# X in token order and block-diagonal C of a chunked scan put into one tile and one load, with another order of the first zero fills, constants and loads

## The chip, the cores and the metric

The kernel is written by hand in Bass/Tile for Trainium2 and runs on one core. A core has five engines that run side by side and tell each other by semaphores when data is ready: TensorE (PE) multiplies matrices and writes to PSUM, VectorE (DVE) and ScalarE (ACT) work on elements, GpSimd (POOL) does slower element work and gathers, SyncE (SP) issues DMAs. Each engine runs its own instructions strictly in order. The metric is device time in microseconds (us) of one execution, lower is better.

## What is computed

Three stages, each fed by the one before: a chunked linear-attention scan, a mixture of experts that sends each token to one of 8 experts, and a wide MLP. The change lies in the first stage alone:

```python
# x (4, 8, 768, 32), a (4, 8, 768), B and C (4, 8, 768, 16); chunk = 32
for c in range(nc):
    sl = slice(c * chunk, (c + 1) * chunk)
    xc, Bc, Cc = (x[:, :, sl], B[:, :, sl], C[:, :, sl])
    la = log_a[:, :, sl]
    cum = np.cumsum(la, axis=-1)
    L = np.exp(cum[:, :, :, None] - cum[:, :, None, :])
    L = L * causal
    CB = np.einsum('bhin,bhjn->bhij', Cc, Bc)
    M = CB * L
    y_intra = np.einsum('bhij,bhjd->bhid', M, xc)
    decay_to_i = np.exp(cum)
    y_inter = np.einsum('bhin,bhnd->bhid', Cc, state) * decay_to_i[:, :, :, None]
    y[:, :, sl] = y_intra + y_inter
    ...
    state = decay_full[:, :, None, None] * state + np.sum(Bx, axis=2)
```

Then `x = y` as 3072 rows of 256, `_moe_ref` (gate, one expert of 256 x 1024 x 256 with relu, gate weight), and `_moe2_ref` (256 x 2048 x 256 with squared relu).

## The kernel before

**Tiling.** The scan's tokens are cut into 24 tiles of 128 tokens, i = 0 to 23, in six phases of four tiles (`ph = i // 4`). Even and odd phases use buffers 0 and 1 of the large tiles. A step, called here by a letter and its tile, is: S(i), L416, the products of C and B for a pair, 16 matmuls into `sc`; M(i), L419, `sc` times the decays `Qm`, on DVE; D(i), L435, 32 matmuls that make the state's update `dS` of two tiles; R(i), L452, eight small recurrences on DVE that make the states `st`; Y(i), L464 (M times x) and L471 (C times state), 16 matmuls each; row(i), L476, on DVE, which scales y into a row tile; then transposes (L493), the gate's logits (L502) and the gate (L526 to L564). `order()`, `gateB`, `spotA` and the like prepare the sending of tokens to experts.

**Operands.** A small matmul contracts over 128 partitions, and four chunks share them, so the operands are block-diagonal: a tile is filled with zeros once, and each phase's load writes only the blocks (`at` in `load_x`, partitions c, c+4, ... in `load_c`). `X2_p` holds X twice, in chunk order ([:, 0], read by Y) and in token order ([:, 1], read by D). `Cb_p` is the block-diagonal C that S reads, `CT_p` (three buffers) the transposed C that Y reads, `BB_p` (three) is B, `Bt_p` the scaled B that D reads and POOL writes in `prep`. A phase is loaded by 15 DMAs on SP: `load_b` 1, `load_x(ph, 1)` 4, `load_c` 4, `load_x(ph, 0)` 4, `load_t` 2. Of these X and C parts have 128 KB each. A load into a buffer waits for the last reader two phases back (for CT and BB, three), and each issue waits for the DMA eight issues before it to land.

**Start.** `aa` (the gates a) is loaded, clamped on DVE (L315), its logarithm taken on ACT (L316). Six matmuls (L331 to L341) make cumulative sums, ACT takes four exponentials of them (Fd, Q, Gm, Pd, L347 to L350), POOL makes Bt (L392) and Qm (L400) from Fd and Q, and D(0) and S(0) can run. The zero fills of phase 0 stand around that on DVE and POOL, those of phase 1 behind it on DVE, ACT and POOL (L631 to L636, L645 to L647).

**Order.** The schedule is by hand (`tc.manual_schedule()`): the order of the code is the order on each engine. The loop over i at L643 works S and D two tiles ahead: PE's order around phase 1 is D(0), S(0), S(1), D(2), Y(0), Y(1), Y(2), S(4), D(4), S(5), Y(3), D(6), Y(4), Y(5), S(8). Nothing of the stages behind waits for a clock time: the experts' weights are staged in the place of `Cb_0` from i = 18 (`ring.stage`, `ring.load`), and after i = 23 PE runs on through the experts and the MLP.

Of the kernel before, what the change touches and what calls it, by code (L numbers as in the profile page):

```python
# [244 lines left out]
def attention(tc, k, ctx):  # L245
# [59 lines left out]
    def zcopy(f, p, b):
        f(Cb[p][:, 2 * b:2 * b + 2].rearrange("p c b e f -> p (c b) (e f)"), zb)

    def xcopy(f, p, l, h):
        f(X2[p][:, l, 2 * h:2 * h + 2].rearrange("p c b f -> p (c b) f"), zb)
# [7 lines left out]
    g.memset(Cb[0][:, 2:4], 0.0)  # L317
    g.memset(X2[0][:, 0, 2:4], 0.0)
    v.memset(Bt[0], 0.0)
    xcopy(v.tensor_copy, 0, 0, 0)  # L320
    v.memset(CT[0][0:64, 1], 0.0)
    v.memset(CT[0][64:128, 0], 0.0)
    load_b(0)
    load_x(0, 1)
    load_c(0)
    load_x(0, 0)
# [1033 lines left out]
```

## Time and profile before

| | us |
|---|---|
| three timed runs | 529.36, 531.80, 532.12 (median 531.80) |
| the profiled execution, its own time | 529.87 |
| its span in the trace | 528.2 |
| PE, DVE, ACT, POOL busy | 503.2, 374.4, 260.9, 107.3 |
| mean granted clock of PE | 0.994 of full |

The span is 1.67 us shorter than the execution's own time. PE is busy nearly throughout, but a busy PE in the scan's part (up to about us 90) often waits for small results of DVE, and the chain of waits, which goes back from the last instruction to what released it each time, tells there what counts. In timelines a line is: start, duration, engine, source line, operation, out<-in, shape, count, and in brackets the idle time before and what ended it. Equal neighbours are merged, so a duration with x2 or more is that of the whole row.

### The profile page before, as it was taken

Reading aid. Unit: us, or ns where it says so; the run is one execution under the profiler, and the core shown is the slowest. Engines: PE = TensorE matmul, PEld = TensorE weight load, DVE = VectorE, ACT = ScalarE, POOL = GpSimd, SP = SyncE. Lnnn points to the kernel's source line nnn. Section 1 sums busy time; section 2 is a strip of 40 time slices with the busy share of each in tenths; the row PEclk is TensorE's granted clock in tenths of the full one; section 3 lists DMA queues with packets and bytes.
Section 4 is the critical chain, followed back from the end, with each engine's and each line's share of the span. In section 5 each row is a group of like instructions: output and inputs, shape, how many; then the busy total and the mean of one; then the engine's idle time right before and its main releaser. Section 6 shows DMA issues by size and latency. Waiting matters only on the chain.

```text
span 528.2 us, 11379 instructions
## 1 busy us (share of the span) xinstructions
PE 503.2 (95%) x4341; PEld 457.5 (87%) x4341; DVE 374.4 (71%) x827; ACT 260.9 (49%) x500; POOL 107.3 (20%) x127
## 2 busy tenths in 40 slices
PE   5978898999999999999999999999999999999994
PEld 3657777989999999999899997999999999999994
DVE  8987988858999899995667777665564555445462
ACT  3612336357565566653554544545454554544552
POOL 6852201443330220000000002002420320201021
PEclk9998999999999999999999999999999999999998
DMA  6777766757878765621001100000100100000010
GB/s 214 222 239 237 231 187 209 232 115 180 215 210 202 194 203 147 213 68 20 1 0 42 41 1 1 1 20 22 61 1 1 41 0 1 31 10 2 1 42 24
DMA packets 35884, 51.22 MB, mean 97 GB/s; under 512 B 7377, under 2 KB 26962, under 8 KB 35826
## 3 DMA queue, kind: packets, MB, share of 16 engines
q1 hardware_dynamic: 32706, 42.88, 28.4%
q0 software_dynamic: 2832, 7.01, 4.5%
q8 instruction: 36, 0.59, 0.4%
q10 hardware_dynamic: 288, 0.55, 0.3%
q14 instruction: 22, 0.18, 0.1%
HBM read 44.06 MB, written 6.37 MB: 95 GB/s over the span
## 4 chain that ended last, share of the span: by engine, by line
PE 69%; DVE 17%; issue 5%; ACT 3%; DMA 2%; POOL 1%; SPq 1%; POOLq 0%; DVEq 0%; ACTq 0%
PE u L1057 23%; PE h L1035 22%; PE h L902 10%; PE o L918 9%; DVE wlo L176 2%; DVE hl L907 2%; DVE st L452 2%; PE tpm L883 1%; DMA wst<-in_w_dram 1%; DMA Cb<-in_cc_dram 1%; PE y L471 1%; PE y L464 1%; DMA CT<-in_ct_dram 1%; POOL out_dram L1070 1%; DVE w L239 1%
## 5 line engine op out<-in xcount | busy, mean ns | idle before, releaser
L1042 DVE TENSOR_TENSOR gb<-q,ga 128x512 fp32r<-128x512 f32 (+1 forms) x112 | 69.6, 622 | 71.4 <-ACT ga L1041 66.4
L1041 ACT ACTIVATE ga<-q 128x512 fp32r<-128x512 f32 (+1 forms) x112 | 63.9, 571 | 99.4 <-DVE q L1040 99.4
L1057 PE MATMUL u<-woh,ga 128*128 128x256 f32 x384 | 108.5, 283 | 1.2 <-ACT ob L1069 0.6
L1057 PE MATMUL u<-wol,ga 128*128 128x256 f32 x384 | 108.1, 281 | 0.0
L1057 PE MATMUL u<-woh,gb 128*128 128x256 f32 x384 | 107.7, 280 | 0.4 <-DVE gb L1042 0.4
L1040 DVE TENSOR_TENSOR q<-r 128x512 f32<-128x512 f32 (+1 forms) x112 | 69.2, 618 | 37.5 <-ACT r L1039 36.5
L1035 PE MATMUL h<-zh,wih 128*128 128x512 f32 (+1 forms) x224 | 81.1, 362 | 0.0
L1035 PE MATMUL h<-zh,wil 128*128 128x512 f32 (+1 forms) x224 | 80.8, 361 | 0.0
L1035 PE MATMUL h<-zl,wih 128*128 128x512 f32 (+1 forms) x224 | 80.7, 360 | 0.0
L1057 PEld LDWEIGHTS u<-woh,ga 128*128 128x128 f32 x384 | 72.1, 188 | 5.9 <-ACT ga L1041 1.7
L1039 ACT ACTIVATE r<-h 128x512 f32<-128x512 f32 (+1 forms) x112 | 59.3, 530 | 33.3 <-PE h L1035 32.5
L1057 PEld LDWEIGHTS u<-wol,ga 128*128 128x128 f32 x384 | 72.1, 188 | 3.1
L1057 PEld LDWEIGHTS u<-woh,gb 128*128 128x128 f32 x384 | 72.5, 189 | 1.3 <-DVE gb L1042 1.2
L905 ACT ACTIVATE hh<-h 128x256 fp32r<-128x256 f32 (+8 forms) x72 | 34.1, 473 | 57.9 <-PE h L902 55.3
L1070 POOL DMA_INDIRECT out_dram<-ob,idx x24 | 24.8, 1033 | 131.4 <-ACT ob L1069 125.6
L1035 PEld LDWEIGHTS h<-zl,wih 128*128 128x128 f32 x224 | 42.1, 188 | 7.3
L907 DVE SCALAR_TENSOR_TENSOR hl<-h,hh 128x256 fp32r<-128x256 f32 (+8 forms) x72 | 38.1, 529 | 14.1 <-ACT hh L905 13.8
L918 PE MATMUL o<-hh,whi 128*128 128x256 f32 (+8 forms) x144 | 47.7, 331 | 0.0
L918 PE MATMUL o<-hh,wlo 128*128 128x256 f32 (+8 forms) x144 | 47.5, 330 | 0.2 <-DVE wlo L176 0.2
L918 PE MATMUL o<-hl,whi 128*128 128x256 f32 (+8 forms) x144 | 47.5, 330 | 0.1
L902 PE MATMUL h<-xh,whi 128*128 128x208 f32 (+7 forms) x128 | 44.6, 348 | 0.8 <-DVE hl L907 0.7
L1035 PEld LDWEIGHTS h<-zh,wil 128*128 128x128 f32 x224 | 42.0, 188 | 3.8
(210 smaller groups left out, 907.7 us busy)
## 6 DMA issues: line engine op xcount, KB each, us to landing
wst<-in_w_dram SPq DMA_DIRECT2D x64, 256.0 KB, 4.8
X<-in_xx_dram SPq DMA_DIRECT2D x48, 128.0 KB, 3.6
w<-in_win_dram SPq DMA_DIRECT2D x8, 512.0 KB, 6.4
w<-in_wout_dram SPq DMA_DIRECT2D x8, 512.0 KB, 3.8
xs<-row SPq DMA_DIRECT2D x6, 516.0 KB, 5.4
BB<-in_bb_dram SPq DMA_DIRECT2D x6, 512.0 KB, 4.7
Cb<-in_cc_dram SPq DMA_DIRECT2D x24, 128.0 KB, 3.6
CT<-in_ct_dram SPq DMA_DIRECT2D x12, 128.0 KB, 3.0
```

Source lines behind the costliest of these rows:

```text
L176: eng.tensor_tensor(lo[:, w], st[:, w], hi[:, w].bitcast(F32), ALU.subtract)
L902: nc.tensor.matmul(ps, ring.up(wt, e, f, kd), xt[:, kd], start=(i == 0), stop=(i == 5))
L905: nc.scalar.activation(a, ps, ACTF.Relu)
L907: rest = lambda: nc.vector.scalar_tensor_tensor(b, ps, 0.0, a.bitcast(F32), ALU.max, ALU.subtract)
L918: nc.tensor.matmul(self.yps[e][d][:, c:c + n], ring.down(wt, e, f, d), ht, start=(f == 0 and i == 0), stop=(f == 7 and i == 2))
L1035: nc.tensor.matmul(ps, wt[:, kd, m * 128:m * 128 + 128], zt[t][:, kd], start=(i == 0), stop=(i == 5))
L1039: nc.scalar.activation(r, ps, ACTF.Relu)
L1040: nc.vector.tensor_tensor(q, r, r, ALU.mult)
L1041: nc.scalar.activation(a, q, ACTF.Copy)
L1042: nc.vector.tensor_tensor(b, q, a.bitcast(F32), ALU.subtract)
L1057: nc.tensor.matmul(o, gt[:, q * 128:q * 128 + 128], wt[:, m], start=(m == 0 and i == 0 and h == 0), stop=(m == 15 and i == 2), skip_group_ ...
L1070: ins = nc.gpsimd.indirect_dma_start(out=k.out, out_offset=bass.IndirectOffsetOnAxis(ap=self.idx[:, c:c + 1], axis=0), in_=ob, in_offset=N ...
```

## The change

X in token order and the block-diagonal C become one DRAM array `xc` and one tile `XC_p` of 128 x 4 x 2048; a part is loaded by one DMA of 256 KB, so a phase has 11 DMAs where it had 15, with the same bytes. X in chunk order has an array `xa` and a tile `XA_p` of its own, 128 x 4 x 1024. The weights' staging takes the place of `XA_0` where it took that of `Cb_0`, and its loads stand at i = 19 instead of 18. The zero fills are dealt out anew: for phase 0 two quarters of `XC_0` to DVE, two to ACT, `XA_0` to POOL and DVE, `Bt_0` to POOL; for phase 1 all four quarters of `XC_1` and the four halves of CT to ACT, `XA_1` and `Bt_1` to POOL. The constants are loaded up to C_ID first, and the rest from ACT's queue behind Pd. The matmul that feeds Pd and Pd itself are a function `decay()`, called behind D(0). All loads of phase 1 stand ahead of the loop; `load_c` of phase ph + 2 comes at i % 4 == 0, `load_b(2)` and `load_t(2)` earlier.

```diff
-    s.dma_start(out=cst[:, 0:C_LO], in_=k.consts[:, 0:C_LO])
-    s.dma_start(out=cst[:, C_LO:C_END], in_=k.consts[:, C_LO:C_END])
+    s.dma_start(out=cst[:, 0:C_ID], in_=k.consts[:, 0:C_ID])
...
+    XC = [bigs[p].tile([128, 4, 2048], F32, name=f"XC_{p}") for p in range(2)]
+    XA = [(big if p else stp).tile([128, 4, 1024], F32, tag=f"XA_{p}", name=f"XA_{p}") for p in range(2)]
+    Xt = [x[:, :, 0:1024].rearrange("p c (b f) -> p c b f", b=2) for x in XC]
+    Cb = [x[:, :, 1024:2048].rearrange("p c (b e f) -> p c b e f", b=2, e=2) for x in XC]
+    Xr = [x.rearrange("p c (b f) -> p c b f", b=2) for x in XA]
...
-            sp.dma_start(out=Cb[p][c:128:4, c], in_=k.cc[ph, c:128:4])
+            sp.dma_start(out=XC[ph % 2][c:128:4, c], in_=k.xc[ph, c:128:4])
...
-    g.memset(X2[0][:, 1, 0:2], 0.0)
-    xcopy(v.tensor_copy, 0, 1, 1)
-    zcopy(v.tensor_copy, 0, 0)
+    load_b(0)
+    blank_c(v.tensor_copy, 0, 0)
+    g.memset(Bt[0], 0.0)
+    blank_c(acopy, 0, 2)
+    g.memset(XA[0][:, 0:2], 0.0)
+    blank_c(v.tensor_copy, 0, 1)
+    blank_c(acopy, 0, 3)
+    load_c(0)
     v.tensor_scalar(aa, aa, 1e-6, 1.0, ALU.max, ALU.min)
     s.activation(la, aa, ACTF.Ln)
...
+    def decay():
+        pe.matmul(cum[:, 1, :192], cst[:, C_WQ:C_WQ + 128], la[:, 1], start=True, stop=True)
+        s.activation(Pd.rearrange("p b t h -> p (b t h)"), cum[:, 1, :192], ACTF.Exp, scale=-1.0)
...
+    prep(0, (0,))
+    st_D(0)
+    decay()
+    s.dma_start(out=cst[:, C_ID:C_END], in_=k.consts[:, C_ID:C_END])
+    load_b(1)
+    for c in range(4):
+        blank_c(acopy, 1, c)
+    load_c(1)
+    prep(0, (1, 2))
+    for h in range(2):
+        g.memset(XA[1][:, 2 * h:2 * h + 2], 0.0)
+    load_x(1)
...
-            load_x(i // 4 + 2, 1)
+            load_c(i // 4 + 2)
...
         if i == 18:
-            k.ring.stage(stp, "Cb_0")
             k.moe = Moe(k, tc, k.c2, m0)
             k.ring.aim(0)
-            k.ring.load(0)
             k.moe.load_rows((0, 0))
...
         if i == 19:
+            k.ring.stage(stp, "XA_0")
+            for n in range(4):
+                k.ring.load(n)
```

ACT's first instructions (zt is the zero tile, Fd, Q, Gm and Pd the four exponentials, in words above), before:

```order
L265 DMA cst<-in_consts_dram 128x899
L266 DMA cst<-in_consts_dram 128x184
L316 ACT_TABLE_LOAD
L316 ACTIVATE aa<-aa 128x576
L347 ACT_TABLE_LOAD
L347 ACTIVATE Fd<-cu_163 128x192
L348 ACTIVATE Q<-cum 128x192
L349 ACTIVATE Gm<-small 128x96
L350 ACTIVATE Pd<-cum 128x192
L311 ACTIVATE Cb_120<-zt 128x2048
L311 ACTIVATE X_1_118<-zt 128x2048 x2
L311 ACTIVATE X_1_118<-zt 128x1024
```

and after:

```order
L264 DMA cst<-in_consts_dram 128x544
L304 ACT_TABLE_LOAD
L304 ACTIVATE XC_116<-zt 128x2048 x2
L326 ACT_TABLE_LOAD
L326 ACTIVATE aa<-aa 128x576
L354 ACT_TABLE_LOAD
L354 ACTIVATE Fd<-cu_166 128x192
L355 ACTIVATE Q<-cum 128x192
L356 ACTIVATE Gm<-small 128x96
L360 ACTIVATE Pd<-cum 128x192
L641 DMA cst<-in_consts_dram 128x539
L304 ACTIVATE XC_117<-zt 128x2048 x4
```

Two zero copies and a third table load came ahead of the logarithm, and four copies for phase 1 (`XC_117` is buffer 1) with a DMA issue stand behind Pd.

SP's queue from the second phase's loads on (`_117`, `_119`, `_124` are buffer 1 after the change; `Cb_119` and `X_0_117` are buffer 0 before it), before:

```order
L281 DMA BB_122<-in_bb_dram 128x1024
L286 DMA Cb_120<-in_cc_dram 32x1024 x4
L292 DMA X_1_118<-in_xx_dram 32x1024 x4
L641 DMA wg<-in_wg_dram 128x64
L292 DMA X_0_117<-in_xx_dram 32x1024 x4
L292 DMA X_1_118<-in_xx_dram 32x1024 x4
L296 DMA CT_125<-in_ct_dram 64x512 x2
L281 DMA BB_123<-in_bb_dram 128x1024
L286 DMA Cb_119<-in_cc_dram 32x1024 x4
```

and after:

```order
L283 DMA BB_121<-in_bb_dram 128x1024
L287 DMA XC_117<-in_xc_dram 32x2048 x4
L292 DMA XA_119<-in_xa_dram 32x1024 x4
L296 DMA CT_124<-in_ct_dram 64x512 x2
L283 DMA BB_122<-in_bb_dram 128x1024
L656 DMA wg<-in_wg_dram 128x64
L296 DMA CT_125<-in_ct_dram 64x512 x2
L287 DMA XC_116<-in_xc_dram 32x2048 x4
```

The third phase's X no longer stands ahead of the second phase's, CT of phase 2 comes ahead of phase 2's C, and four issues fewer stand in the row.

PE's first instructions, before:

```order
L331 MATMUL cu_163<-aa,cst 128x192
L334 MATMUL cu_163<-aa,cst 128x4x40
L336 MATMUL cum<-aa,cst 128x192
L337 MATMUL cum<-aa,cst 128x192
L340 MATMUL small<-aa,cst 128x96
L341 MATMUL small<-aa,cst 128x4x23
L435 MATMUL dS_129<-X_0_117,Bt_127 32x4x32 x8
L435 MATMUL dS_130<-X_0_117,Bt_127 32x4x32 x8
L416 MATMUL sc<-Cb_119,BB_121 32x256 x16
```

and after:

```order
L339 MATMUL cu_166<-aa,cst 128x192
L342 MATMUL cu_166<-aa,cst 128x4x40
L344 MATMUL cum<-aa,cst 128x192
L347 MATMUL small<-aa,cst 128x96
L348 MATMUL small<-aa,cst 128x4x23
L442 MATMUL dS_128<-XC_116,Bt_126 32x4x32 x8
L442 MATMUL dS_129<-XC_116,Bt_126 32x4x32 x8
L359 MATMUL cum<-aa,cst 128x192
L423 MATMUL sc<-XC_116,BB_120 32x256 x16
```

The second matmul into `cum` (that of Pd) moved behind D(0).

## Rows read from the trace of the kernel before

**Rows 1.** The page: shares of the chain of waits by engine.

```profile
PE 69%; DVE 17%; issue 5%; ACT 3%; DMA 2%; POOL 1%; SPq 1%; POOLq 0%; DVEq 0%; ACTq 0%
```

**Rows 2.** Chain of waits, first 10 us: start, duration, what.

```profile
3.73 2.82 DVE Cb L306
6.56 2.07 DVE aa L315
8.64 0.69 ACT aa L316
9.38 1.01 PE cu L331 x2
```

**Rows 3.** Timeline of PE: start, duration, line, operation, count, idle time before.

```profile
11.36 0.85 PE L337 MATMUL cum<-aa,cst 128*128 128x192 f32 x2
12.93 1.20 PE L435 MATMUL dS<-X,Bt 128*32 128x128 f32 x32
...
21.35 1.05 PE L416 MATMUL sc<-Cb,BB 128*32 128x256 f32 x16
...
28.75 0.65 PE L464 MATMUL y<-X,M 128*32 128x128 f32 x16 [0.96 <-DMA X<-in_xx_dram]
...
33.44 1.07 PE L416 MATMUL sc<-Cb,BB 128*32 128x256 f32 x16 [1.78 <-DMA Cb<-in_cc_dram]
...
43.72 0.50 PE L471 MATMUL y<-st,CT 128*32 128x128 f32 x8 [0.92 <-DMA CT<-in_ct_dram]
```

**Rows 4.** Timeline of ACT and of its DMA queue, first 20 us.

```profile
1.27 0.45 ACTq L266 DMA_DIRECT2D cst<-in_consts_dram  x1
...
9.35 1.28 ACT L347 ACT_TABLE_LOAD   x1
...
13.18 0.33 ACT L350 ACTIVATE Pd<-cum 128x192 f32<-128x192 f32 x1
13.39 1.92 ACT L311 ACTIVATE Cb<-zt 128x2048 f32<-128x2048 f32 x1
15.19 4.66 ACT L311 ACTIVATE X<-zt 128x2048 f32<-128x2048 f32 x3
```

**Rows 5.** Timelines of DVE (first row) and POOL (the others), zero fills.

```profile
9.61 1.16 DVE L309 COPY X<-zt 128x2048 f32<-128x2048 f32 x1
2.59 2.88 POOL L317 MEMSET Cb<- 128x2048 f32 x1
...
16.55 1.81 POOL L636 MEMSET X<- 128x2048 f32 x1
```

**Rows 6.** DMA issues of us 6.5 to 13, then 77 to 84: count, KB each, median to landing.

```profile
Cb<-in_cc_dram SPq DMA_DIRECT2D x4, 128.0 KB, 2.5
...
wst<-in_w_dram SPq DMA_DIRECT2D x8, 256.0 KB, 5.8
```

**Rows 7.** Timeline of DVE: row(5), M(8), M(12), M(16).

```profile
31.47 0.43 DVE L476 TENSOR_TENSOR row<-y,Pd 128x256 f32<-128x256 f32 x1 [0.88 <-PE y L471]
...
34.64 0.69 DVE L419 TENSOR_TENSOR M<-sc,Qm 128x512 f32<-128x512 f32 x1 [0.39 <-POOL Qm L400]
...
48.53 0.68 DVE L419 TENSOR_TENSOR M<-sc,Qm 128x512 f32<-128x512 f32 x1
...
60.17 0.68 DVE L419 TENSOR_TENSOR M<-sc,Qm 128x512 f32<-128x512 f32 x1
```

**Rows 8.** Stretches: length, busy us of PE, PEld, DVE, ACT, POOL, granted clock, DMA share, GB/s.

```profile
30.00:34.00 4.00, 2.22 (x65) 1.74 (x61) 2.85 (x9) 0.61 (x3) 3.21 (x8) 1.00 0.88 265
40.00:44.00 4.00, 2.65 (x46) 2.10 (x50) 2.75 (x10) 1.44 (x3) 0.00 (x0) 0.99 0.52 155
44.00:47.00 3.00, 3.00 (x57) 2.50 (x45) 0.78 (x3) 0.28 (x1) 0.00 (x0) 0.50 0.90 266
```

**Rows 9.** Timelines of PE (Y(19)) and of SP's queue (first weight load).

```profile
77.02 0.62 PE L464 MATMUL y<-X,M 128*32 128x128 f32 x16
...
77.54 0.42 SPq L161 DMA_DIRECT2D wst<-in_w_dram  x1
```

More of the change, by code (lines that the diff above doesn't have):

```diff
@@ L283, in load_c, with load_x @@
     def load_c(ph):
-        p = ph % 2
         for c in range(4):
-            sp.dma_start(out=Cb[p][c:128:4, c], in_=k.cc[ph, c:128:4])
-    def load_x(ph, l):
-        p = ph % 2
+            sp.dma_start(out=XC[ph % 2][c:128:4, c], in_=k.xc[ph, c:128:4])
+    def load_x(ph):
         for c in range(4):
-            at = slice(c, 128, 4) if l else slice(32 * c, 32 * c + 32)
-            sp.dma_start(out=X2[p][at, l, c], in_=k.xx[ph, at, l])
+            at = slice(32 * c, 32 * c + 32)
+            sp.dma_start(out=XA[ph % 2][at, c], in_=k.xa[ph, at])
     def load_t(ph):
@@ L303, in attention, with blank_c, blank_x, zero_t @@
     la = aa
[L305 to L309, printed above, removed]
     acopy = lambda o, i: s.activation(o, i, ACTF.Copy)
-    g.memset(X2[0][:, 1, 0:2], 0.0)
-    xcopy(v.tensor_copy, 0, 1, 1)
-    zcopy(v.tensor_copy, 0, 0)
+    def blank_c(f, p, c):
+        f(XC[p][:, c].rearrange("p (a f) -> p a f", f=512), zb)
+    def blank_x(f, p, half):
+        f(XA[p][:, 2 * half:2 * half + 2].rearrange("p c (b f) -> p (c b) f", f=512), zb)
+    def zero_t(f, p):
+        for h in range(2):
+            o = CT[p][64 * h:64 * h + 64, 1 - h].rearrange("p a f -> p (a f)")
+            f(o, zt[64 * h:64 * h + 64])
+    load_b(0)
[6 more added lines that the diff above has]
+    load_c(0)
     v.tensor_scalar(aa, aa, 1e-6, 1.0, ALU.max, ALU.min)
     s.activation(la, aa, ACTF.Ln)
[L317 to L326, printed above, removed]
+    blank_x(v.tensor_copy, 0, 1)
+    load_x(0)
+    zero_t(v.tensor_copy, 0)
     load_t(0)
+    states = {}
+    for b in range(4):
+        states[b, 0] = pl3.tile([128, 4, 128], F32, tag="st", name="st", bufs=8)
+        v.memset(states[b, 0][:, 0], 0.0)
     cum = ps_s.tile([128, 2, 256], F32, tag="sc", name="cum")
@@ L336, in attention @@
     pe.matmul(cum[:, 0, :192], cst[:, C_WQ:C_WQ + 128], la[:, 0], start=True, stop=True)
-    pe.matmul(cum[:, 1, :192], cst[:, C_WQ:C_WQ + 128], la[:, 1], start=True, stop=True)
     l3 = la[:, 2].rearrange("p (b c f) -> p b c f", b=4, c=24)
@@ L371, in attention, with prep @@
     mk = cst[:, C_MASK:C_MASK + 32]
-    scs, Ms, ys, rows, states = {}, {}, {}, {}, {}
-    for b in range(4):
-        states[b, 0] = pl3.tile([128, 4, 128], F32, tag="st", name="st", bufs=8)
-        v.memset(states[b, 0][:, 0], 0.0)
-    def zero_t(f, p):
-        for h in range(2):
-            o = CT[p][64 * h:64 * h + 64, 1 - h].rearrange("p a f -> p (a f)")
-            f(o, zt[64 * h:64 * h + 64])
+    Ms, rows = {}, {}
     Qms = {}
-    def prep(ph):
+    def prep(ph, parts=(0, 1, 2)):
         g_, pr = divmod(ph, 2)
@@ L392, in bt, with qm @@
                 g.tensor_tensor(Bt[p][:, t2, b2, :, 0:4:3, :], src, fb, ALU.mult)
-        if ph == 0:
-            bt(0)
-        for j in range(2):
+        def qm(j):
             b = 2 * pr + j
@@ L403, in prep @@
             Qms[ph, j] = q
-            if ph or j:
+        if ph:
+            for j in range(2):
+                qm(j)
                 bt(j)
+            return
+        for part in parts:
+            bt(0) if part == 0 else qm(part - 1)
+        if 2 in parts:
+            bt(1)
     def st_S(i):
@@ L1287, in kernel_body @@
 @with_exitstack
-def kernel_body(ctx, tc, consts, aa, xx, cc, bb, ct, wg, w1, w2, win, wout, out):
+def kernel_body(ctx, tc, consts, aa, xa, xc, bb, ct, wg, w1, w2, win, wout, out):
     nc = tc.nc
@@ L1338, in kernel_body @@
         rest(tc, k)
-_NAMES = ["consts", "aa", "xx", "cc", "bb", "ct", "wg", "w1", "w2", "win", "wout"]
+_NAMES = ["consts", "aa", "xa", "xc", "bb", "ct", "wg", "w1", "w2", "win", "wout"]
 def kernel(**inputs):
```

49 lines of the change are left out of this document (13 added, 36 removed).

## The prediction

> **What bounds the kernel now.** I read the shares of the chain of waits first. PE holds 69% of it and DVE 17%, DMA only 2% [rows 1]; the experts and the MLP behind the scan are matmul after matmul, and the change does not touch them, so whatever it moves by the end of the scan's part is carried to the end of the span as it is. The question is therefore how much earlier or later the scan ends. In the start of the chain the reader is to see four links: zero copies on DVE (the second of 2.82 us), the clamp of `aa` behind them, the logarithm on ACT at 8.64, the first cumulative matmul at 9.38 [rows 2]. PE's timeline then has three waits for DMAs: 0.96 us for X before Y(4), 1.78 us for C before S(8), 0.92 us for CT in Y(8) [rows 3]. [...] Phases 3 to 5 have no such wait. So the change can win about the start, and in phases 1 and 2; it can lose wherever a new wait stands in front of one of these.
>
> **The start: 1.0 us earlier.** DVE copies of 128x2048 take 1.16 us alone, but 2.82 us while POOL fills [rows 2, 5]: the two engines take turns, each for a whole instruction (POOL's fill is 2.88 us then, 1.81 alone). With one POOL fill of that size instead of three, DVE is through its two copies and the clamp by about 6.2 us, an estimate from these rows: 1.8 (POOL's half-size fill) + 1.16 + 1.8 + 1.16 + 0.3. ACT is later than that and decides. It starts 0.45 us sooner, one DMA issue less, at 1.3 [rows 4]; a table load of 1.28, two copies (1.80 from start to start, 1.92 for the last: 3.72), a second table load of 1.28 end at 7.6; the logarithm, 0.69, at 8.3 [rows 2, 4]. The first cumulative matmul goes at 8.34, 1.04 us before the old 9.38.
>
> [...]
>
> **D(0): 1.7 us earlier.** It began at 12.93, 3.55 after the first matmul, behind L337, which moves away; from 11.36 to the next start the row gives about 0.64 [rows 3]. 8.34 + 3.55 - 0.64 = 11.25. The four loads of XC_0 don't hold it: the last can be issued by 7.1, and even with a landing of 3.5 us it is there at 10.6.
>
> **The new wait, S(4): 2.75 us later.** S(4) ran at 21.35 [rows 3]. It now reads XC_1, whose four quarters are all filled by ACT, in order, behind Pd; and Pd waits for a matmul that stands behind D(0). D(0) 1.20 gives 12.45, the matmul 0.64, Pd 0.33, the constants' issue 0.45: the first copy starts at 13.85 [rows 3, 4]. Four copies are 3 x 1.80 + 1.92 = 7.32, to 21.2. Then SP can issue the last quarter. For its landing the near rows are 2.5 us (128 KB, quiet queue) and 5.8 us (256 KB, in 1 KB pieces, beside a gather) [rows 6]; I take 2.9, near the first, because SP has nothing else in flight then but the quarter before, issued 1.8 us earlier. S(4) starts at 24.1. Bounds: 23.7 by the quick landing; 28.0 by 5.8 us and by a D(0) that takes 1.0 us more, if it runs at the low clock. Behind S(4) in PE's order wait D(4), S(5), Y(3), D(6) and Y(4), behind M(4) all of DVE; behind the quarter on SP wait XA_1 and CT. PE has nothing to do from about 19.4, when Y(2) is through. Before, copies for phase 1 were shared by DVE, POOL and ACT, and none of this showed.
>
> **Phase 1 to M(8): 0.7 us later.** Row(5) ran at 31.47, 10.12 after S(4), of which 0.96 was the wait for X [rows 3, 7]. XA_1 now lands at about 27, CT_1 at 28, eight issues of 0.6 us behind the quarter, before Y(4) needs them (about 30.5), so that wait falls out: 2.75 - 0.96 = 1.8 later. PE was free for S(8) at 31.66 and waited 1.78; now it is free at 33.46, just the old 33.44. XC_0's load for phase 2 is issued by 29.5 and lands by about 33: the stall turns into lateness, no more. M(8) followed row(5) by 3.17 with 0.39 of waiting [rows 7]; full DVE work gives 33.27 + 2.78 = 36.05 (+1.4), PE alone gives +0.0, and I take +0.7, the middle.
>
> **Phase 2: 2.25 us won.** M(8) to M(12) took 13.89 us, M(12) to M(16), the same work without a DMA wait, 11.64 [rows 7]. The difference is the wait for CT and the slow stretch behind it. CT for phase 2 is now issued ahead of phase 2's C, some 14 us before its reader. M(12) is then 1.55 earlier.
>
> **The clock in phase 1: 1.2 us lost.** PE's clock fell to 0.50 after a stretch in which PE was busy 2.65 of 4 us with a wait at its end; with 2.22 of 4 us, spread out, it stayed at 1.00 [rows 8]. [...] S(4) and D(4), 2.0 us together at full clock, gate DVE; doubled they cost 2.0 more, at full clock nothing. I take 1.2.
>
> **The rest.** The weights' staging now needs Y(19) to have read XA_0: that row starts at 77.02 and lasts 0.62, and SP issued the first weight load at 77.54 [rows 9]; 0.1 us is lost. Four issues fewer in a phase cost and win nothing where no load was late; the packets carry the same bytes. DVE's 2.0 us of zero fills less in phase 0 stand in the wait for S(4).
>
> **Sum.** +0.7 - 2.25 + 1.2 + 0.1 = -0.25 us. The profiled execution, 528.2 of span and 1.67 around it, would take 529.87 - 0.25 = 529.6. The four executions shown (three timed, one profiled) have 530.8 as their median; carried there the forecast is 530.5. That is no change; 0.5%, 2.7 us, is about what a measurement of this kernel can tell.
>
> **Rivals.** (1) Faster: the three waits and the slow stretch go at full size and the new wait is small. They are 0.96 + 1.78 + 0.92 + about 1.3 = 5.0 us; S(4) at 23.7 costs 2.35, and the clock stays up: -2.65, or 528.1; with D(0) quicker too, -3.3 or 527.5. For it: phases 3 and 4 show that DVE and PE can run without waits. Against: four ACT copies in a row are plain in the order. (2) Slower: the landing of XC_1's last quarter decides. Each us of it is a us at the end once the stall of S(8) is used up, as it is here. At 5.8 us, and with D(0) at the low clock, S(4) is at 28.0 and the total 3.9 worse: 534.4. It decides from S(4) at about 27 on. Against it: nothing competes for the queues at that moment. [...] (4) The change does not do what it says: loads in larger pieces win nothing because they were never late, and CT's wait is replaced by another fall of the clock in phase 2, +1.3: 531.8.
>
> **How the numbers follow.** Forecast 0.50, faster 0.25, slower 0.15, the drain 0.04, the fall of the clock in phase 2 0.06. The last two stay within 0.5%. That gives faster 0.25, same 0.59, slower 0.16, some of rival 4 lying beyond the bound. The range for 8 in 10 takes the forecast's bounds, 528.4 to 532.5, and reaches into both rivals: 527.6 to 533.2.
>
> **What would show it.** In the changed kernel's trace: the logarithm at 8.3 and D(0) at 11.2; four ACT copies from 13.9 to 21.2; PE idle for some 4 to 5 us before S(4) at 24.1, ended by the DMA of XC; a granted clock of 0.50 somewhere between 21 and 28; no wait for a DMA before Y(4), S(8) and in Y(8); M(8) to M(12) about 11.6 us. I am wrong if S(4) starts before 22.5 or after 27, or if phase 2 is still 13 us long.

## The result and the profile after

The changed kernel takes 534.19 us (median of 20 runs, 531.45 to 535.37), the kernel before 529.99 us (20 runs); the ratio is 1.0063, with an interval of 1.0045 to 1.0081. The forecast was 530.5 us with a range to 533.2: it was wrong in sign and size, and the time lies outside the range. A repeat in another set gave 1.0051 [1.0030, 1.0073], a third 1.0043 [1.0007, 1.0078]; on one chip the ratio was 0.9989 (below).

Where it went is read best from the times at which DVE starts the M's (timelines of DVE; S(4) from PE's), us:

| kernel | S(4) | M(4) | M(8) | M(12) | M(16) | M(20) | M(21) | span |
|---|---|---|---|---|---|---|---|---|
| before | 21.35 | 22.54 | 34.64 | 48.53 | 60.17 | 73.39 | 78.81 | 528.2 |
| after | 25.99 | 28.05 | 38.03 | 50.38 | 62.22 | 77.06 | 82.57 | 533.5 |
| after, repeat (r1_same) | 26.93 | 28.99 | 38.86 | 50.37 | 62.48 | 76.03 | 81.62 | 531.1 |
| r2_dve_fills | 23.30 | 24.48 | 34.18 | 45.85 | 58.25 | 71.83 | 77.24 | 527.0 |
| r3_decay_early | 24.77 | 26.79 | 37.50 | 48.36 | 60.68 | 74.52 | 79.92 | 529.9 |
| r4_both | 23.61 | 24.80 | 34.82 | 46.70 | 60.20 | 73.54 | 78.95 | 528.9 |
| r16_half_turn | 21.78 | 22.98 | 32.78 | 44.61 | 56.90 | 69.31 | 74.71 | 525.5 |

M(21) is 3.76 us late, and the span is 5.3 us longer; the profiled execution (535.31 us) lies 1.1 us over the median. In the repeat M(21) is 2.81 late and the span 2.87 longer: the loss is that of the scan, as the forecast had it ("carried to the end as it is"), and the further 1.5 us of the first trace did not come again.

The start, ACT's timeline (start, duration, line, operation, idle time before), to be held against [rows 2, 4]:

```profile
2.59 3.71 ACT L304 ACTIVATE XC<-zt 128x2048 f32<-128x2048 f32 x2
6.33 1.28 ACT L326 ACT_TABLE_LOAD   x1
7.62 0.68 ACT L326 ACTIVATE aa<-aa 128x576 f32<-128x576 f32 x1
8.32 1.28 ACT L354 ACT_TABLE_LOAD   x1
...
11.36 0.25 ACT L356 ACTIVATE Gm<-small 128x96 f32<-128x96 f32 x1 [0.46 <-PE small L348]
14.90 0.33 ACT L360 ACTIVATE Pd<-cum 128x192 f32<-128x192 f32 x1 [3.28 <-PE cum L359]
14.91 0.34 ACTq L641 DMA_DIRECT2D cst<-in_consts_dram  x1
15.29 7.32 ACT L304 ACTIVATE XC<-zt 128x2048 f32<-128x2048 f32 x4
```

Look at Pd, for which ACT sits idle for 3.28 us, and at the four copies that cannot begin before it. PE's timeline, against [rows 3]:

```profile
8.36 1.01 PE L339 MATMUL cu<-aa,cst 128*128 128x192 f32 x2 [3.15 <-ACT aa L326]
...
11.99 1.94 PE L442 MATMUL dS<-XC,Bt 128*32 128x128 f32 x32 [0.66 <-DMA XC<-in_xc_dram]
13.86 1.01 PE L359 MATMUL cum<-aa,cst 128*128 128x192 f32 x2
14.79 2.09 PE L423 MATMUL sc<-XC,BB 128*32 128x256 f32 x32
...
25.99 1.94 PE L423 MATMUL sc<-XC,BB 128*32 128x256 f32 x16 [4.03 <-ACT xt L503]
27.67 1.63 PE L442 MATMUL dS<-XC,Bt 128*32 128x128 f32 x32
...
36.82 1.07 PE L423 MATMUL sc<-XC,BB 128*32 128x256 f32 x16 [0.55 <-DMA XC<-in_xc_dram]
...
54.10 0.83 PE L442 MATMUL dS<-XC,Bt 128*32 128x128 f32 x22
56.20 0.60 PE L442 MATMUL dS<-XC,Bt 128*32 128x128 f32 x10 [1.27 <-issue]
...
61.59 0.40 PE L442 MATMUL dS<-XC,Bt 128*32 128x128 f32 x7
64.44 0.95 PE L442 MATMUL dS<-XC,Bt 128*32 128x128 f32 x25 [2.45 <-issue]
```

S(4) waited 4.03 us. The releaser printed there is the last of several: PE's queue first waited for the DMA of XC's last quarter, issued at 22.64 and landed at 25.64, and went on at 25.67; ACT's xt ended at 25.69. New, and in no rival of the forecast, are the two pauses in the middle of D(14) and D(16), 1.27 and 2.45 us, that end at nothing the trace names ("issue"). The waits for X before Y(4) and for CT in Y(8) are gone; that of S(8) has shrunk from 1.78 to 0.55 us. SP's issues of XC_1 (four, from first start to last end), then the granted clock (the column behind POOL's; columns as in [rows 8]) before and in S(4):

```profile
17.24 5.87 SPq L287 DMA_DIRECT2D XC<-in_xc_dram  x4
```

```profile
21.00:25.40 4.40, 0.96 (x32) 0.69 (x29) 0.42 (x1) 4.33 (x6) 2.51 (x6) 1.00 0.60 183
```

```profile
25.40:28.80 3.40, 2.81 (x40) 2.06 (x44) 0.69 (x1) 0.29 (x1) 0.00 (x0) 0.50 0.83 189
```

PE, busy 0.96 of 4.4 us ahead of it, does S(4) and D(4) at a granted clock of 0.50, in 1.94 and 1.63 us. DVE, against [rows 7], is late at row(5) by 4.6, at M(8) by 3.4, at M(12) by 1.85 and at M(16) by 2.05 us:

```profile
36.08 0.43 DVE L483 TENSOR_TENSOR row<-y,Pd 128x256 f32<-128x256 f32 x1 [0.48 <-PE y L478]
...
38.03 0.69 DVE L426 TENSOR_TENSOR M<-sc,Qm 128x512 f32<-128x512 f32 x1 [0.24 <-PE sc L423]
...
50.38 0.68 DVE L426 TENSOR_TENSOR M<-sc,Qm 128x512 f32<-128x512 f32 x1
...
62.22 0.68 DVE L426 TENSOR_TENSOR M<-sc,Qm 128x512 f32<-128x512 f32 x1
```

And the page's shares of the chain, against [rows 1], where "issue" (idle time whose end the trace explains by nothing) and ACT have grown at the cost of PE and DVE:

```profile
PE 64%; DVE 14%; issue 7%; ACT 6%; DMA 4%; POOL 3%; SPq 2%; POOLq 0%; ACTq 0%; DVEq 0%
```

### The profile page after: what moved, and what is told of

Its sections match the earlier page's. It is cut to its first block, busy times and chain, and to the rows that moved or that the text cites. A ratio compares the mean times of both kernels' runs of the same rounds, so it can differ in the third digit from the quotient of the medians.

```text
span 533.5 us, 11338 instructions
## 1 busy us (share of the span) xinstructions
PE 504.6 (95%) x4341; PEld 458.3 (86%) x4341; DVE 366.9 (69%) x822; ACT 268.6 (50%) x505; POOL 103.9 (19%) x127
## 4 chain that ended last, share of the span: by engine, by line
PE 64%; DVE 14%; issue 7%; ACT 6%; DMA 4%; POOL 3%; SPq 2%; POOLq 0%; ACTq 0%; DVEq 0%
PE u L1057 20%; PE h L1035 19%; PE h L902 9%; PE o L918 8%; DVE wlo L175 2%; DVE q L1040 2%; DVE hl L907 2%; DMA wst<-in_w_dram 2%; ACT ga L1041 2%; DVE gb L1042 1%; PE sc L423 1%; PE dS L442 1%; PE y L471 1%; POOL Qm L399 1%; DMA XC<-in_xc_dram 1%
## 5 line engine op out<-in xcount | busy, mean ns | idle before, releaser
L907 DVE SCALAR_TENSOR_TENSOR hl<-h,hh 128x256 fp32r<-128x256 f32 (+8 forms) x72 | 38.2, 530 | 13.5 <-ACT hh L905 13.2
```

The costliest lines, as they stand in the source:

```text
L907: rest = lambda: nc.vector.scalar_tensor_tensor(b, ps, 0.0, a.bitcast(F32), ALU.max, ALU.subtract)
```

## Experiments: the wait at S(4)

Theory A: the loss is the wait at S(4), made by four fills of XC_1 in a row on ACT, behind Pd, behind a matmul that stands behind D(0). Theory B: a large part are the pauses of PE in D. Runs of one set ran on one chip; the kernel before took 530.99 us in this one.

**r1_same**, the changed kernel again.

> The changed kernel once more, unaltered. Theory A (the loss is the new wait at S(4), and what follows from it): S(4) starts at about 26.0 us and M(8) at about 38 us again, so the first expert matmul stays about 3.8 us later than before. Theory B (a large part of the loss is the two pauses of PE in the middle of D at 56.2 and 64.4 us, 1.27 and 2.45 us, for which the trace names no releaser): if the pauses belong to this program they come again at the same instructions with about the same length; if they are chance, they are gone and M(16) to M(20) is about 12 us instead of 14.8. The part behind 93 us, where the profiled execution lost 1.5 us more, should be about 0.3 us, since the median lies 1.1 us below that execution. Time 534 us by both.

Measured: 533.98 us, 1.0051 [1.0030, 1.0073]. S(4) came at 26.93 after 3.82 us of waiting. The pause in D(16) came again at the same product, with 0.56 us; that in D(14) did not, and one of 0.80 us came 256 instructions behind the first, in D(18): the places belong to the program, the lengths do not. Of 2.8 us lost, 1.8 are there by M(12); the pauses, 1.4 us, are enough to cover the rest.

**r2_dve_fills.**

```diff
     for c in range(4):
-        blank_c(acopy, 1, c)
+        blank_c(v.tensor_copy if c < 2 else acopy, 1, c)
```

> Of the four fills of XC_1, the first two go to DVE, which has nothing to do from 8.6 to 13.2 us, and ACT keeps two. Theory A: ACT's last copy ends 3.6 us earlier (at about 19.0 instead of 22.6), the last quarter lands at about 22.0, S(4) starts at about 22.3, M(4) at about 23.6 instead of 28.05, and PE's idle time before S(4) falls under 0.6 us, so the clock stays at 1.00 there. Of the 3.8 us that are lost by the first expert matmul 3 to 4 come back: about 530.5 us. Theory B (the pauses of PE in D, at 56 and 64 us): the pauses stay, M(12) to M(20) remains about 2 us longer than before, and no more than 2 us come back: 532 us or more. Theory C (a joined load of 256 KB lands late whatever the fills): the landing takes 5 us, S(4) is at about 24 and 2 us come back: 532 us.

Measured: 530.73 us, 0.9990 [0.9964, 1.0016]: 3.2 us came back against r1_same, all of the loss. In PE's timeline S(4) follows Y(2) without idle time, at a clock of 1.00:

```profile
22.86 0.62 PE L478 MATMUL y<-st,CT 128*32 128x128 f32 x16
23.30 1.05 PE L423 MATMUL sc<-XC,BB 128*32 128x256 f32 x16
...
46.62 0.64 PE L442 MATMUL dS<-XC,Bt 128*32 128x128 f32 x15 [0.68 <-issue]
...
52.24 0.60 PE L442 MATMUL dS<-XC,Bt 128*32 128x128 f32 x10 [0.87 <-issue]
...
58.91 0.95 PE L442 MATMUL dS<-XC,Bt 128*32 128x128 f32 x25 [0.88 <-issue]
```

Theory C falls (the last quarter, issued at 19.02, landed at 22.22). Theory A holds: without the late fills the wait and the loss are gone. The pauses of B stay, 2.4 us in all, in a kernel that has won its time back.

**r3_decay_early.** The matmul for Pd back with the other cumulative ones, Pd behind Gm.

```diff
+    pe.matmul(cum[:, 1, :192], cst[:, C_WQ:C_WQ + 128], la[:, 1], start=True, stop=True)
     Q = cp.tile([128, 4, 24, 2], F32, name="Q")
...
     st_D(0)
-    decay()
```

> The matmul that feeds Pd stands with the other cumulative ones again, ahead of D(0), and Pd right behind Gm. Theory A: Pd starts at about 11.9 instead of 14.9, the four ACT copies run from about 12.4 to 19.7, the last quarter lands at about 22.8, S(4) starts at about 23.1, 2.9 us sooner, and the time is about 531.3 us. D(0), which waits for the load of XC_0 at 11.99, stays where it is. If the place of the matmul did not matter (theory A false: ACT copies not on the path), S(4) stays at 26 and the time at 534.

Measured: 530.66 us, 0.9985 [0.9958, 1.0013]. ACT's copies ran from 12.63 to 19.95, as expected; the last quarter landed 4.45 us after its issue, so S(4) came at 24.77 and not at 23.1:

```profile
24.77 1.91 PE L421 MATMUL sc<-XC,BB 128*32 128x256 f32 x16 [3.48 <-DMA XC<-in_xc_dram]
```

The other half of theory A's chain holds too: Pd's place moved the copies and S(4). But S(4) is still 3.4 us later than in the kernel before, and the time is that of the kernel before: M(8) to M(12) took 10.86 us in this trace, the least of all. So how the loss divides between the wait and what varies behind it is not shown.

**r4_both**, the two edits together.

> Both edits: two of XC_1's fills on DVE, and the matmul for Pd and Pd in their old places. Theory A: ACT's two copies end at about 16.0, the last quarter lands at about 19, S(4) follows Y(2) without a wait at about 21.9 (21.35 before), and the time is 530 us, the same as before within 0.5 us, or 1 us below if the waits of phase 2 stay away as well (M(8) to M(12) 12.4 us against 13.9). Theory B: the pauses of PE in D near 52 and 60 us stay, M(12) to M(20) is about 2 us longer than before, and the time is 532 us.

Measured: 531.37 us, 1.0007 [0.9981, 1.0034]: no more than either alone. Y(0) found a new wait:

```profile
19.44 0.43 PE L476 MATMUL y<-st,CT 128*32 128x128 f32 x8 [2.56 <-DMA CT<-in_ct_dram]
```

The second part of the constants, now issued at 11.98 from ACT's queue, had taken the slot, and the semaphore, of CT's second half, which SP could issue at 15.06 (10.08 in r2_dve_fills), just behind the landing of the constants at 15.04. That is what `decay()` behind D(0) had kept away. The pauses were 0.53, 0.82, 0.87, 1.33 and 0.55 us.

## Experiments: the pauses in D

Counted in the trace, PE's instructions where it pauses stand 256 apart, or a multiple of it (in the first trace of the changed kernel it goes on at its instructions 1729 and 1985, counted from 0 with weight loads and semaphore instructions). The page has a DMA queue of kind "instruction" with 36 packets and 0.59 MB, that is 16 KB each, or 64 bytes for each of 256 instructions. In the first traces of both kernels, from 15 to 78 us, the most frequent number of data packets in flight is 15 while one of these 16 KB moves, and 16 while no packet of kind "instruction" does: the 16 KB take a place that data would take. The times of these packets, against PE's (worked out from the packed traces, us):

```
run            turn before   16 KB moved     PE goes on   after the end
after          50.11         53.50-54.84     56.20        1.36
after          56.20         61.85-63.02     64.44        1.42
r1_same        54.63         60.05-61.20     62.59        1.39
r2_dve_fills   39.74         43.98-45.07     46.62        1.55
r2_dve_fills   46.62         49.66-50.76     52.24        1.48
r16_half_turn  41.87         45.79-47.05     48.53        1.48
```

A turn is here the point at which PE has begun its next 256 instructions; the lag is the time from a turn to the start of the 16 KB that PE needs at the turn after it. The 16 KB begin to move up to 5.7 us after the turn here and take 1.1 to 1.3 us, and PE goes on 1.4 to 1.6 us after their end. From turn to turn the scan takes 6.0 us (median; 4.4 to 10.3), so what lag PE can bear depends on when it gets to the next turn. In the 18 traces without split loads, from the fourth to the ninth turn, all 27 pauses over 0.45 us that end within 1.6 us of such a transfer came with a lag of 2.96 us or more, while 4.53 us passed without one in r15_best_again, where the next turn came 8.8 us later. In the first trace of the kernel before the lags at the six turns between 34 and 66 us were 0.4 to 3.1 us without such a pause; the closest was the turn at 59.57, whose 16 KB ended 1.36 us before the next.

The next set ran on a chip where the kernel before took 538.08 us.

**r5_split.**

```diff
-            sp.dma_start(out=XC[ph % 2][c:128:4, c], in_=k.xc[ph, c:128:4])
+            for at in (slice(0, 1024), slice(1024, 2048)):
+                sp.dma_start(out=XC[ph % 2][c:128:4, c, at], in_=k.xc[ph, c:128:4, at])
```

> The changed kernel with each 256 KB load of XC issued as two of 128 KB (X half, C half), nothing else altered. In the traces so far PE pauses in D only where a turn of 256 of its instructions is full, 1.3 to 1.5 us after the next 16 KB of its program have come by DMA, and these 16 KB come up to 5.7 us after the turn before. Theory B1 (the pauses come from the joined loads: with eight DMAs outstanding twice the bytes lie in front of the program's 16 KB): with 128 KB loads the time from issue to landing of loads near 50 to 60 us falls from about 8 back to about 5 us, the pauses fall under 0.4 us in all, M(8) to M(20) is under 37.5 us (39.0 in the first trace, 37.2 in the repeat), and 0.8 to 2 us come back: about 532.5 us. Theory B2 (the order and place of the loads, not their size): the pauses stay, 534 us or, with four more issues in a phase, more. The wait at S(4) stays near 4 us by both; its start moves by less than 0.7 us.

Measured: 539.11 us, 0.9997 [0.9968, 1.0025]; the unaltered kernel had 0.9989 on this chip (r9_same_b). Pauses of 1.57 and 1.85 us stayed. Theory B1 falls: the joined load is not their cause, and its size costs and wins nothing here.

**r6_fills_split**, the edit of r2_dve_fills on top.

> Two fills of XC_1 on DVE and the loads of XC split in two. Theory A with B1: neither the wait at S(4) nor the pauses in D (0.68, 0.87 and 0.88 us with the fills alone) remain; the time is 1 to 2 us below that with the fills alone: about 529.3 us, faster than before by 0.3%. By B2 the pauses stay and the time is 530.7 us or more.

Measured: 537.19 us, 0.9979 [0.9956, 1.0003], with pauses of 2.97 and 1.49 us, and S(4) waited 3.85 us again: with twice the issues SP issued nothing of XC_1 from 15.1 to 18.96 us. The issue at 18.96 waited, by its semaphore, for the constants that ACT had issued at 13.91 and that landed at 18.95: the slot of r4_both again.

**r7_filler.**

```diff
             st_Y(2)
+            for _ in range(4):
+                pe.matmul(dS[0].rearrange("p a b -> p (a b)"), zt[:, 0:128], zt, start=True, stop=True)
```

> The changed kernel with four needless products of zeros (128x512, about 0.9 us each) on PE between Y(2) and S(4), in the time in which PE only waits. They show what the granted clock is worth there. If the fall to 0.50 costs what the trace suggests (S(4) 1.94 and D(4) 1.63 us against 1.05 and 0.87), S(4) starts at 26.0 to 26.3 again, M(5) comes 1.0 to 1.4 us after what it was relative to S(4) (5.2 us, then 3.9), and the time is about 532.8 us. If the clock's fall is without effect on the end, 534 us.

Measured: 538.53 us, 1.0005 [0.9983, 1.0027]. The clock stayed at 1.00; PE's rows, first with the filler, then without it (r9_same_b, same chip):

```profile
22.58 3.70 PE L662 MATMUL dS<-zt 128*128 128x512 f32 x8
26.30 1.07 PE L423 MATMUL sc<-XC,BB 128*32 128x256 f32 x16
27.16 1.08 PE L442 MATMUL dS<-XC,Bt 128*32 128x128 f32 x32
```

```profile
26.17 1.94 PE L423 MATMUL sc<-XC,BB 128*32 128x256 f32 x16 [3.94 <-DMA XC<-in_xc_dram]
27.83 1.95 PE L442 MATMUL dS<-XC,Bt 128*32 128x128 f32 x32
```

M(5) came 3.9 us after S(4), against 5.5: 1.6 us, of which 0.85 were left at M(8), and nothing shows in the time. The clock's fall is real and not what the result hangs on.

**r8_before_ct**, the kernel before with CT of phase 2 early.

```diff
             load_b(2)
             load_c(2)
-        if i == 4:
             zero_t(acopy, 2)
             load_t(2)
```

> The kernel before, with one thing of the change alone: CT for phase 2 is zeroed and loaded two tiles earlier, right behind C for phase 2. The forecast took 2.25 us for the wait for CT in Y(8) (0.92 us) and the slow stretch behind it. If that is its size, M(8) to M(12) falls from 13.9 to about 11.7 us, the granted clock stays at 1.00 from 44 to 47 us, and the time is 2 us lower, about 529 us. If only the wait goes: 0.9 us. If SP's queue passes the wait on (C or X of phase 2 late instead), nothing.

Measured: 537.84 us, 0.9988 [0.9967, 1.0009]: nothing. M(8) to M(12) was 12.35 us, but the unaltered kernel before on this chip took 11.32 there (r12_before_b), without any wait for CT. And PE paused 2.52 us in D at 54.70, the clock at 0.50 behind it: M(12) to M(16) took 16.5 us. The wait that the forecast counted was that of one execution, and in this trace more was lost at a late turn than the wait was worth.

The third set, same chip, the kernel before at 538.02 us:

**r9_same_b**, unaltered.

> The changed kernel unaltered, as the measure for the other runs of this set: 1.005 times the kernel before, S(4) at 26 to 27 us, PE pauses in D at turns of 256 instructions that add up to 1.4 to 3.7 us between 40 and 70 us.

Measured: 537.26 us, 0.9989 [0.9966, 1.0012], not 1.005; S(4) at 26.17, one pause over 0.45 us (0.52). In the scan the changed kernel is behind here as well (M(21) at 82.33, 80.88 in r12_before_b), and the kernel before loses something else behind it.

**r10_fewer_bytes.**

```diff
-        for c in range(4):
+        for c in range(4 if ph < 3 else 1):
```

> The changed kernel without three of the four XC loads of phases 3 to 5 (0.75 of 2.8 MB in each; their D, S and all behind them run on stale data, so only the scan's times mean anything). The next 16 KB of PE's program come by the same DMA engines as the data. Theory B (they come late because data is in front of them): with fewer bytes in flight they come within 2 us of the turn, the pauses in D from 45 us on vanish (under 0.3 us in all), and M(12) to M(20) falls from 26.7 (first trace) and 25.7 us (repeat) to 24.5 or less. Rival (the pauses come from PE or from the program's memory, whatever the data loads do): they stay at 1.4 us or more.

Measured: M(12) to M(20) 24.3 us (25.1 in r9_same_b), but the lag at the turn of 55.05 was 5.07 us, and a pause of 1.15 us stayed at 62.71 (another, of 0.79 at 38.58, lies ahead of the stretch asked for). XC's bytes alone are not what the 16 KB wait for; a row write and BB, issued at 53.80 and 54.30, were still in front of that turn. (Its time, 617 us, goes with stale data and tells nothing.)

**r11_best**, the two edits of r4_both, and the constants issued elsewhere:

```diff
     load_t(0)
+    sp.dma_start(out=cst[:, C_ID:C_END], in_=k.consts[:, C_ID:C_END])
...
-    s.dma_start(out=cst[:, C_ID:C_END], in_=k.consts[:, C_ID:C_END])
```

> Two fills of XC_1 on DVE, the matmul for Pd and Pd in their old places, and the second part of the constants issued by SP behind CT of phase 0. With both edits alone the constants had gone out ahead of CT's second half, which then waited for their landing, and Y(0) lost 2.56 us. Theory A: CT of phase 0 lands at about 14.5, Y(0) does not wait, XC_1's last quarter is issued at about 16 and lands at 19 to 20, S(4) runs at 20 to 20.5 (21.35 before), M(8) at about 32.5; the time is 0.3 to 0.5% under the kernel before. Theory B (from about 40 us on PE cannot go faster than the next pages of its program come in between the data): the pauses in D grow by what is won ahead of them, and the time is that of the kernel before within 0.1%.

Measured: 532.99 us, 0.9906 [0.9873, 0.9938], and 0.992 of r9_same_b. S(4) ran at 21.30 after 1.05 us of waiting, M(8) at 32.09. About 0.6% of the ratio is the kernel before's own loss on this chip (r12_before_b). Both theories had a part: three pauses of 2.53, 1.94 and 2.17 us took back 6.6 us of this execution's scan (M(21) at 80.64).

**r12_before_b**, the kernel before, unaltered.

> The kernel before, unaltered, once more with a trace, on the chip of this set. In its first trace no pause of PE in D was over 0.45 us, and M(12) to M(20) took 24.9 us. If the pauses are a matter of the change alone they are absent here too; if they belong to any order whose loads come close together they appear here at the same turns of 256 instructions, smaller than in the changed kernel.

Measured: 540.33 us; PE paused 0.74 us in D at 52.11, so the pauses are not the change's own. This trace of the kernel before is 10.4 us longer than its first, 8.3 us of that behind M(21): 457.7 us from there to the end, 449.4 in the first trace. About 3 us seem to be the chip's, since the changed kernel and its variants have them too: 452.3 to 454.8 us on this chip and on that of the next section, 449.4 to 451.0 on the others (r10_fewer_bytes left out); their cause is open. The rest is the kernel before's own, and ACT's rows show it:

```profile
102.77 0.38 ACT L905 ACTIVATE hh<-h 128x256 fp32r<-128x256 f32 x1 [0.52 <-PE small L737]
109.33 0.66 ACT L905 ACTIVATE hh<-h 128x256 fp32r<-128x256 f32 x2 [6.18 <-remote]
```

and in PE's:

```profile
110.22 0.95 PE L883 MATMUL tpm<-cst,xr 128*128 128x128 f32 x4 [3.77 <-DVE hl L907]
```

The clock was at 0.50 from 109 to 116 us. The same is in the trace of r8_before_ct (6.39 us, at the same instruction), and no pause of that size is in those of the changed kernel and its variants on that chip. If the timed runs have it too, as their 538 us suggest (530, about 3 for the chip and 4 to 5 for this), it is why the ratio is 0.9989 here and not 1.005. A packet of another "instruction" queue ended at 107.8, 1.5 us before ACT went on; that ACT waits there for its own program, and that the change moved ACT's turn, fits but was not tested.

## Experiments: moving the lag, moving the turns

Another chip, the kernel before at 537.28 us; all three are r11_best with one edit or none.

**r13_rows_late.** In `gateB` the write of the rows is put off to behind `load_t` of the phase:

```diff
+    later = []
...
-        sp.dma_start(out=k.xs[1 + 128 * i:1 + 128 * (i + n), :].rearrange("(r p) c -> p r c", p=128), in_=row4)
+        def send():
+            sp.dma_start(out=k.xs[1 + 128 * i:1 + 128 * (i + n), :].rearrange("(r p) c -> p r c", p=128), in_=row4)
+        if i < 12:
+            later.append(send)
+        else:
+            send()
...
             load_t(nx)
+        if i % 4 == 3:
+            while later:
+                later.pop()()
```

> The kernel of the last set (two fills on DVE, Pd early, constants by SP), and the write of the rows of phases 0 to 2 (516 KB in rows of 1032 bytes) issued behind CT of the phase instead of ahead of BB, 4 to 6 us later. In the fourteen traces so far the 16 KB of program that follow a turn came 4 us or more after it 19 times, and 15 of these turns had a row write issued 0.4 to 3.6 us ahead. Theory B4 (a turn right behind a row write waits longest): the turns near 41 and 53 us get their 16 KB within 3.5 us, the pauses in D near 48 and 61 us (1.94 and 2.17 us in that kernel) fall under 1 us each, and the time is 0.2 to 0.5% under that kernel. Rival (any load that is in front does the same): the lag stays at 4 to 5.5 us, the pauses stay over 1.5 us, and the time is that of that kernel within 0.15%.

Measured: 531.53 us, 0.9904 [0.9876, 0.9932], the same as r15_best_again. The lags at 38.2 and 49.7 us were 4.22 and 7.85 us with the row write out of the way, and PE paused 2.84 us: theory B4 falls, and its rival, that any load in front does the same, fits better. Ahead of the turn at 49.7 stood four loads of XC, issued from 46.15 to 49.55.

**r14_shift.**

```diff
+    for _ in range(64):
+        pe.matmul(small[:, 480:512], zt[:, 0:128], zt[:, 0:32], start=True, stop=True)
     cum = ps_s.tile([128, 2, 256], F32, tag="sc", name="cum")
```

> The same kernel with 64 tiny products of zeros (128x32) on PE in its idle time at 5 to 8 us: 128 more instructions, so each turn of 256 instructions comes 128 instructions, some 2.8 us, earlier in the schedule; nothing else moves. If the pauses are made by late program, they move: PE stops at other instructions than the 23rd and 24th product of D (turn + 256), half a turn earlier. If they belong to D's operands, they stay at the same products of D. The time is within 0.3% of that kernel; the granted clock may be 1.00 for D(0), which takes 1.05 instead of up to 1.94 us then.

Measured: 556.25 us, 1.0368 [1.0317, 1.0420]. A miss of mine: 64 products were 256 instructions, a whole turn, and took 27 us, so the scan started 24 us late and the turns stayed at their places. It tells nothing of the turns.

**r15_best_again.**

> The kernel of the last set once more, as the measure for these two, and for the ratio to the kernel before. There the kernel before lost some 7 us near 102 to 116 us, where ACT paused 6.2 us and PE's clock fell, which it did not in its first trace; where that loss is absent, the ratio should be 0.995 to 1.000 by theory B (three pauses in D of 6.6 us in all took back what was won ahead of them), where it is present, 0.99.

Measured: 531.79 us, 0.9911 [0.9878, 0.9943]; of the kernel before there is no trace on this chip. This kernel's trace has one pause of 1.10 us and M(21) at 77.52, 3.1 us sooner than the same program in r11_best.

The last set, a chip where the kernel before took 531.20 us:

**r16_half_turn.**

```diff
+    for n in range(32):
+        pe.matmul(small[0:32, 480:512], zt[:, 0:32], zt[:, 0:32], start=(n == 0), stop=(n == 31))
     cum = ps_s.tile([128, 2, 256], F32, tag="sc", name="cum")
```

> In the last set the 64 products were 256 instructions (each is two passes of a weight load and a product), a whole turn, and took 27 us: the turns stayed at their places in the schedule. Here 32 products of 32x32 weights are put in PE's idle time at 5 to 8 us, 128 instructions and some 2 to 4 us (D's products of that size: 32 passes in 1.05 to 1.94 us), nothing else: each turn of 256 comes half a turn sooner in the schedule. If the pauses are made by late program, they move: with the same lags of up to 4.5 us PE stops half a turn away from the products of D where it stopped, and the sum of its pauses may go up or down; the first cumulative product comes up to 0.8 us late if the clock is at 0.50. If the pauses belong to D's operands, they stay at the same products of D. The time is 530 to 534 us where the kernel without the shift takes 532.

Measured: 528.92 us, 0.9953 [0.9922, 0.9983]: the fastest of all against a kernel before of 531 us, below the 530 to 534 us expected, and 0.991 of the changed kernel in the same set. What the shift alone is worth is not shown, since r11_best did not run on this chip. The products took 2.38 us, and the clock stayed at 1.00 through the whole scan, as it did without them in r13_rows_late. The pause moved from D into S:

```profile
46.59 0.61 PE L424 MATMUL sc<-XC,BB 128*32 128x256 f32 x7
48.53 0.81 PE L424 MATMUL sc<-XC,BB 128*32 128x256 f32 x9 [1.33 <-issue]
```

**r17_quarter_turn**, 16 products.

> The same with 16 such products: 64 instructions, a quarter of a turn. Turns come 64 instructions sooner in the schedule than without the shift, so any pause comes at the instruction where the count, less 193, is a multiple of 256, not at the place in D it has without the shift. The time is 530 to 534 us.

Measured: 530.05 us, 0.9964 [0.9937, 0.9991]; the pause stood in Y, after 9 of the 16 passes of its second half:

```profile
58.45 0.42 PE L479 MATMUL y<-st,CT 128*32 128x128 f32 x7 [1.05 <-issue]
```

With both, the pauses are shown to be the turns of PE's program and not D's operands.

**r18_same_c**, unaltered.

> The changed kernel unaltered, on the chip of this set. Where the kernel before takes 531 us (no pause of ACT near 102 to 116 us) the ratio is 1.005; where the kernel before takes 537 us or more it is 0.998. S(4) starts at 26 to 27 us in either.

Measured: 533.66 us, 1.0043 [1.0007, 1.0078], S(4) at 25.60, a pause of 1.10 us: on the three chips where the kernel before takes 530 to 531 us, the change loses 0.4 to 0.6%.

What the 16 KB wait for stays open in part. In 18 traces (those with split loads left out) the turns from the fourth to the ninth have 108 lags, of up to 7.9 us. They go with the bytes that SP has issued and that have not yet moved at the turn (issues' sizes against the packets of SP's queue that have ended): all 23 lags of 4 us or more had 0.88 MB or more in front. With less than that, at 67 turns, the median lag was 2.0 us and the longest 3.5; with that or more, at 41 turns, the median was 4.1 us and the shortest 1.4. Neither the loads' size, nor XC's bytes, nor the place of the row write was it alone: where one of them was taken away, others were in front. That fewer bytes of any kind in front would take the pauses away is the likeliest reading, and no run tested it.

## Why the prediction was wrong

The mechanism of the new wait was right; its size and two other terms were not. At M(21) the sum has -0.25 us where 3.8 were lost. It lacks 1.5 us up to M(8), since D(0) and with it the copies and S(4) came later than forecast; 1.9 us in phases 3 to 5, where "Phases 3 to 5 have no such wait" put at nothing what PE's pauses took; and 0.7 us in phase 2, whose gain was taken from one execution.

- **The start** held: logarithm at 7.62 to 8.30 (8.3 forecast), first matmul at 8.36 (8.34). The third table load cost 1.28 us and no more: ACT's next row starts 0.01 us behind it, and the load at 8.32 starts where the logarithm ends. The drain to which the forecast gave 0.04, more time lost around a table load, did not show.
- **D(0)**: 11.99 (12.92 in the repeat) instead of 11.25. The step that failed first is "even with a landing of 3.5 us it is there": the last quarter of XC_0, issued at 6.89, took 4.97 us, PE waited 0.66. Then D(0) took 1.94 and the matmul for Pd 1.01 us at a clock of 0.50, where I had 1.20 and 0.64 from rows of the kernel before. Pd was 1.8 us later than forecast.
- **The new wait, S(4)**: the mechanism was right link by link (four copies in 7.32 us exactly, landing 3.0 for 2.9 us, between the ends of [rows 6], idle time 4.0, clock at 0.50, S(4) released by XC). Its size was not: 4.64 us (5.58 in the repeat) where the sum has 2.75, since it inherited the lateness of D(0): the first copy began at 15.29 instead of 13.85, 1.44 of the 1.89 us; the rest came between the last copy and S(4). Rival (2) "decides from S(4) at about 27 on" and gave 534.4 us; it came true at 26 to 27, through the half of its condition that I had priced at 1.0 us (D(0) late and slow), not by the landing. That its 534.4 us lie beside the measured 534.19 is luck: it had S(4) at 28.0, and it had no pauses of PE.
- **Phase 1 to M(8)**: 3.4 us late (4.2 in the repeat) where 0.7 and 1.2 for the clock make 1.9. Row(5) was as late as S(4), 4.6 us: the vanished wait for X had given 0.96 us, and the slow clock is the likely taker. The 1.2 us for the clock were my estimate, between nothing and a doubling of S(4) and D(4), 2.0 us; no run shows that figure, and 1.6 us at M(5) and 0.85 at M(8) were measured in its place (r7_filler against r9_same_b).
- **Phase 2**: 12.35 us from M(8) to M(12), 11.51 in the repeat; the gain of 1.5 to 2.4 us against 2.25 was there. But r12_before_b shows 11.32 us in the kernel before as well: I had taken one execution's wait for a property of the kernel.
- **Phases 3 to 5**: forecast unchanged, measured 1.9 us (1.0 in the repeat) longer from M(12) to M(21), with pauses of 3.7 (1.4) us at PE's turns in it. This cause was in no rival: I counted the waits that the trace of before showed, and in it the 16 KB came in time at every turn, once with nothing to spare.
- **The staging of the weights**: the first issue was 3.92 us late, M(21) 3.76: 0.16 for 0.1 us. The first matmul of the experts is 3.78 us late. Right.

Sum by what was measured at M(21): +3.4 to M(8), -1.5, +1.9, in all 3.8 us, against the forecast's +1.9, -2.25, 0 (and +0.1 for the staging). The bounds of 528.4 to 532.5 us, from which the range was made, follow from no line of the working, and rival (2) lay outside that range.

## What to carry to other kernels

When a step is moved behind another, carry every late link into it at its worst row, clock included: three small ones (0.74, 0.74 and 0.37 us) made Pd 1.8 us late, and the new wait 1.9 us longer than forecast. A chain of fills on one engine that ends in a load is cut from either end, and one end is enough until the next wait shows. In a kernel with many small matmuls, look for pauses that stand a constant count of an engine's instructions apart (256 of PE's here) before blaming operands, and compare several traces before counting on a wait.

## What was not expected of the hardware

- In these traces PE stopped at turns of 256 instructions when 16 KB of its program came late: lags of up to 7.9 us, pauses of 0.5 to 3.0 us, 1.3 to 1.7 us from the end of the transfer to the next instruction. Needless instructions ahead, half or a quarter of a turn of them, moved the pauses, to S at 48.53 us (r16_half_turn) and to Y at 58.45 us (r17_quarter_turn). Lags of 4 us or more came only with 0.88 MB or more of loads issued and not yet moved.
- The same two programs rank differently on different chips: 1.0063, 1.0051 and 1.0043 in three sets, 0.9989 on another chip, where the two traces of the kernel before (one with an edit) have a pause of ACT of 6.2 and 6.4 us with the clock at 0.50 behind it, and those of the changed kernel have none.
